# A check summed over partitions by VectorE block transposes instead of fp32 matmuls, with a fallback branch of seven transfers

## Chip, cores, metric

One Trainium2 chip, one core. The metric is device time in microseconds (us) of one execution. The kernel of before had a median of 1509.73 us in three runs (1509.59 to 1510.04).

## The reference, cut to what matters

```python
def _A_ref(x, mem0, Wq, Wk, Wv, Wo, seg_len):   # x 1 x 2048 x 1024, 64 segments of 32 tokens
    mem = mem0                                   # 8 memory rows
    for s in range(n_seg):
        h = concat([mem, xs]);  q, k, v = h @ Wq, h @ Wk, h @ Wv      # 32 heads of 128
        p = softmax(where(mask, q k^T * scale, -1e9))
        o = (p @ v) @ Wo
        mem = o[:, :M]                           # memories of the next segment
        outs.append(o[:, M:])

def _B_ref(x, w1, w2, w3, w4):
    h = gelu(layernorm(x) @ w1);  x1 = x + shift(h) @ w2
    return x1 + gelu(layernorm(x1) @ w3) @ w4

xn = layernorm(x)
return x + _A_ref(xn, ...) + _B_ref(xn, ...)
```

The recurrence over 64 segments is serial. The kernel guesses all memories beforehand, computes every segment in parallel, and at the end compares the memories that come out with the guesses. If they differ, a branch at the end does the serial computation. For these inputs the guesses hold, and the branch is never taken.

## The kernel before

These are the parts that the change and the argument touch. First the constants and the helper that sums squares over partitions with a matmul by ones:

```python
    def load_consts(n):
        for _ in range(n):
            t, d = const_loads.pop(0)
            nc.gpsimd.dma_start(t[:], d.ap())

    ident = const_tile("c_ident", np.eye(P, dtype=np.float32))
    load_consts(1)
    ...                                     # four more: eye9, mask_first, mask_reg, mask_two

    def row_norms(pool, ppool, tag, src, in_place=False):
        sq = src if in_place else pool.tile([P, KT, NQ], F32, tag="nsq", bufs=1)
        nc.vector.tensor_tensor(sq[:], src[:], src[:], op=ALU.mult)
        sr = pool.tile([P, NQ], F32, tag="nsr", bufs=1)
        nc.vector.tensor_reduce(sr[:], sq[:].rearrange("p k r -> p r k"), axis=AX.X, op=ALU.add)
        ps = ppool.tile([P, 512], F32, tag=tag)
        nc.tensor.matmul(ps[:1, :NQ], ones_f[:], sr[:], start=True, stop=True)      # L163
        return ps
```

The start. Every token tile is normalised, then transposed: tiles 0 to 5 by TensorE, tiles 6 to 15 by a DMA transpose on SyncE's queue (L278).

```python
    def load_w3():                          # 0.9 MB each
        ...
        nc.sync.dma_start(w3_sb[:, 2 * k0:2 * k0 + 2, cs], w3_v[:, 2 * k0:2 * k0 + 2, cs])

    for n in range(7, 10):
        load_x(n)                           # nc.sync.dma_start, 0.25 MB each
    def norm_stats(n, part=None):
        ...
        nc.gpsimd.tensor_tensor(rr[:], ab[:], neghalf[:], op=ALU.pow)               # L265
    def norm2(n, xn2T, jj):
        ...                                 # DVE for n < 8, else ACT (L276)
        if n >= NPE:                        # NPE = 6
            nc.sync.dma_start_transpose(xn2T[:, jj], xn2[:])                        # L278
    def norm1(n):
        ...
        if n < 3:
            load_x(n + 10)
        if n in (12, 15):
            load_w3()
    ...
    load_consts(4)
    for n in range(1, 6):
        ...
    for n in range(13, NT):
        load_x(n)
    def prep(n):
        norm2_of(n)
        norm_stats(n + 1)
        norm1(n - 2)
    for n0 in range(4, NT, 2):
        ...                                 # stage1(n0, 2, ...): matmuls by w1, L318
    for n in (NT - 2, NT - 1):
        norm1(n)
```

The middle and the tail:

```python
    def unit_thr():                         # between two units of the value stage
        ps = row_norms(ring, psum3, "vr", GT)
        nc.vector.tensor_scalar(gthr[:], ps[:1, :NQ], TOL2, None, op0=ALU.mult)
    ...
    bad = smp.tile([P, 1], F32, tag="bad", bufs=1)      # 1 where a softmax sum is out of range
    ...
    for o in rest[:2]:
        for p in range(8):
            o.piece(p)                      # output matmuls, L725
    psd = row_norms(iop, apsum, "S", Dm, in_place=True) # Dm = memories - guesses
    okf = smp.tile([1, NQ], F32, tag="okf", bufs=1)
    nc.vector.tensor_tensor(okf[:], psd[:1, :NQ], gthr[:], op=ALU.is_le)
    ...
    nc.tensor.matmul(psc[:1, :1], bad[:], ones_f[:], start=True, stop=True)         # L886
    ...
    for o in rest[2:]:
        for p in range(8):
            o.piece(p)

    cond = nc.values_load(flag_i[0:1, 0:1], min_val=0, max_val=NQ + P)
    with tc.If(cond > 0):                   # L896: 29 transfers
        nc.sync.dma_start(wo_sb[:], Wo_v)
        nc.sync.dma_start(mask40[:], mask40_d.ap())
        with tc.For_i(0, NSEG, 1) as i:
            ...                             # xs, Rt, 8 x (wq, wk, wv) in eighths, out
```

## Time and profile before

| quantity | before | where from |
|---|---|---|
| time, three runs | 1509.73 us (1509.59 to 1510.04) | timed runs |
| span of the profiled run | 1508.1 us | top of the page |
| TensorE busy | 1498.3 us, 99% | table of busy time |
| start: first transpose to first matmul by w2 | 59.46 us | starts of the records |
| first matmul by w3 to first value matmul | 410.74 us | starts of the records |
| attention: first score matmul (L682) to the check's first matmul (L865) | 701.82 us | starts of the records |
| last stage: the check's matmuls to the last matmul | 36.27 us | starts of the records |
| last matmul to the end | 4.07 us | starts of the records |

The busy table is read first: an engine at 99% leaves the others nothing to decide except at the start and behind its last instruction.

### The profile page before, as it was taken

Reading aid. Unit: us, or ns where it says so; the run is one execution under the profiler, and the core shown is the slowest. Engines: PE = TensorE matmul, PEld = TensorE weight load, DVE = VectorE, ACT = ScalarE, POOL = GpSimd, SP = SyncE. Lnnn points to the kernel's source line nnn. Section 1 sums busy time; section 2 is a strip of 40 time slices with the busy share of each in tenths; the row PEclk is TensorE's granted clock in tenths of the full one; section 3 lists DMA queues with packets and bytes.
Section 4 is the critical chain, followed back from the end, with each engine's and each line's share of the span. In section 5 each row is a group of like instructions: output and inputs, shape, how many; then the busy total and the mean of one; then the engine's idle time right before and its main releaser. Section 6 shows DMA issues by size and latency. Waiting matters only on the chain.

```text
span 1508.1 us, 24241 instructions
## 1 busy us (share of the span) xinstructions
PE 1498.3 (99%) x9762; PEld 803.5 (53%) x9834; DVE 544.6 (36%) x1136; ACT 501.9 (33%) x1140; POOL 175.6 (12%) x246
## 2 busy tenths in 40 slices
PE   9999999999999999999999999999999999999998
PEld 8744444445444444444456645664665455545555
DVE  8382230100020212221146624651564166516641
ACT  6433103013012011111256614650663266416630
POOL 5241020211111221100000010001000100010001
PEclk9999999999999999999999999999999999999999
DMA  9599762353355787622389956992998299919911
GB/s 313 155 254 329 220 180 88 133 203 113 126 164 147 195 250 253 212 98 84 126 223 254 244 125 175 257 239 68 247 244 203 74 227 228 212 62 200 216 49 51
DMA packets 305380, 272.93 MB, mean 181 GB/s; under 512 B 156023, under 2 KB 272281, under 8 KB 305265
## 3 DMA queue, kind: packets, MB, share of 16 engines
q1 hardware_dynamic: 282800, 189.38, 50.5%
q0 software_dynamic: 21776, 80.85, 15.6%
q8 instruction: 79, 1.29, 0.4%
q10 hardware_dynamic: 688, 1.11, 0.2%
q14 instruction: 37, 0.30, 0.1%
HBM read 190.08 MB, written 45.29 MB: 156 GB/s over the span
## 4 chain that ended last, share of the span: by engine, by line
PE 97%; DVE 1%; DMA 1%; issue 0%; POOL 0%; ACT 0%; SPq 0%; POOLq 0%
PE ps L667 30%; PE pso L725 15%; PE ps L601 15%; PE ps L542 13%; PE ps L568 13%; PE ps L400 4%; PE ps L318 2%; PE psS L682 2%; PE psO L706 2%; PE ps L865 1%; PE ps L492 1%; PE gps L471 0%; PE ps L457 0%; DMA wt<-in_A_Wq_dram 0%; DVE st L262 0%
## 5 line engine op out<-in xcount | busy, mean ns | idle before, releaser
L667 PE MATMUL ps<-hTb,wt 128*128 128x396 bf16 (+2 forms) x2528 | 485.0, 342 | 0.1
L667 PEld LDWEIGHTS <-wt 128*128 128x128 bf16 x2528 | 236.7, 98 | 175.8 <-DMA wt<-in_A_Wq_dram 0.5
L601 PE MATMUL ps<-wt,xT 128*128 128x512 bf16 x1003 | 220.1, 379 | 1.1
L725 PE MATMUL pso<-wo_sb,oX 128*128 128x512 bf16 (+1 forms) x972 | 208.5, 372 | 1.1
L542 PE MATMUL ps<-xn3T,w_sb 128*128 128x512 bf16 x896 | 196.2, 379 | 0.0
L568 PE MATMUL ps<-w_sb,h3T 128*128 128x512 bf16 x873 | 194.3, 379 | 1.2
L601 PEld LDWEIGHTS <-xT 128*128 128x128 bf16 x1024 | 100.2, 98 | 120.8
L543 ACT ACTIVATE h3T<-ps 128x512 bf16<-128x512 f32 x112 | 66.8, 597 | 290.4 <-PE ps L542 289.5
L725 PEld LDWEIGHTS <-oX 128*128 128x128 bf16 x992 | 96.3, 98 | 107.4
L669 ACT CAST KT<-ps 128x462 bf16<-128x462 f32 (+2 forms) x160 | 81.7, 510 | 203.0 <-PE ps L667 198.8
L568 PEld LDWEIGHTS <-h3T 128*128 128x128 bf16 x896 | 87.0, 98 | 103.4
L542 PEld LDWEIGHTS <-w_sb 128*128 128x128 bf16 x896 | 86.6, 98 | 102.0
L688 DVE TENSOR_REDUCE sums<-sm 99x4 f32<-99x396 f32 (+2 forms) x176 | 97.6, 555 | 114.9 <-ACT sm L686 114.9
L671 ACT ACTIVATE QT<-ps 128x462 bf16<-128x462 f32 (+2 forms) x160 | 83.8, 524 | 120.6 <-PE ps L667 106.6
L603 ACT CAST Vs<-ps 128x512 bf16<-128x512 f32 x64 | 37.5, 585 | 233.2 <-PE ps L601 174.9
L684 DVE TENSOR_TENSOR sm<-psS,c_mask_reg_sb 99x396 f32<-99x396 f32 x152 | 86.7, 570 | 71.7 <-PE psS L682 71.4
L607 DVE CAST Vs<-ps 128x512 bf16<-128x512 f32 x64 | 44.3, 692 | 171.6 <-PE ps L601 163.2
L686 ACT ACTIVATE sm<-sm 99x396 f32<-99x396 f32 (+2 forms) x176 | 92.8, 527 | 35.0 <-DVE sm L684 28.2
L694 DVE TENSOR_TENSOR Pn<-sm,rs 99x396 bf16<-99x396 f32 (+2 forms) x176 | 98.9, 562 | 7.1 <-DMA PT<-Pn 0.8
L732 POOL DMA_DIRECT2D out_dram<-ot x30 | 16.4, 546 | 698.9 <-DVE ot L731 693.0
L569 DVE TENSOR_TENSOR R<-ps,R 128x512 f32<-128x512 f32 x32 | 21.9, 689 | 175.3 <-PE ps L568 154.9
L731 DVE TENSOR_TENSOR ot<-pso,Rt 128x512 bf16<-128x512 f32 (+1 forms) x33 | 22.3, 675 | 170.4 <-PE pso L725 166.2
(123 smaller groups left out, 1048.3 us busy)
## 6 DMA issues: line engine op xcount, KB each, us to landing
wt<-in_A_Wq_dram SPq DMA_DIRECT2D x76, 512.0 KB
wt<-in_A_Wk_dram SPq DMA_DIRECT2D x76, 512.0 KB
wt<-in_A_Wv_dram POOLq DMA_DIRECT2D x24, 1024.0 KB, 6.5
V_scratch<-Vs SPq DMA_DIRECT2D x32, 512.0 KB
V<-V_scratch SPq DMA_DIRECT2D x40, 384.0 KB
R_scratch<-x POOLq DMA_DIRECT2D x16, 512.0 KB, 4.7
R<-R_scratch SPq DMA_DIRECT2D x16, 512.0 KB
R_scratch<-R POOLq DMA_DIRECT2D x16, 512.0 KB, 3.8
```

The source lines that it names most:

```text
L542: nc.tensor.matmul(ps[:].rearrange("p (n t) -> p n t", t=P), w3_sb[:, k, f * P:(f + 1) * P], xn3T[tb][:, :, k, :], start=(k == 0), stop=(k ...
L543: nc.scalar.activation(h3T[:, f, :], ps[:], ACTF.Gelu_apprx_tanh)
L568: nc.tensor.matmul(ps[:], h3T[:, f, j * P:(j + 1) * P], w4_sb[:, f, ch * 512:(ch + 1) * 512], start=(f == 0), stop=(f == FT - 1))
L601: nc.tensor.matmul(ps[:], xT[:, m4 * 4 + j, k, :], wv[:, k, :], start=(k == 0), stop=(k == KT - 1))
L667: nc.tensor.matmul(ps[:, :nb], w[:, k, hh * P:(hh + 1) * P], B["hT"][:, k, :nb], start=(k == 0), stop=(k == KT - 1))
L669: nc.scalar.copy(dst[:, hh, :], ps[:, :nb])
L671: nc.scalar.mul(dst[:, hh, :], ps[:, :nb], scale)
L684: nc.vector.tensor_tensor(sm[:T, :, :T], S3, t["mask"][:].unsqueeze(1).to_broadcast((T, 4, T)), op=ALU.add)
L686: nc.scalar.activation(e[:T, :, :T], sm[:T, :, :T], ACTF.Exp, scale=LN2)
L688: nc.vector.tensor_reduce(ss, e[:T, :, :T], axis=AX.X, op=ALU.add)
L694: nc.vector.tensor_tensor(Pn[:T, :, :T], e[:T, :, :T], rs[:T, :].unsqueeze(2).to_broadcast((T, 4, T)), op=ALU.mult)
L725: nc.tensor.matmul(self.ps[:, :self.w], self.oX[0][:, h, self.oX[1] + self.gl * P:self.oX[1] + (self.gl + 1) * P], wo_sb[:, h, self.cc], s ...
```

## The change

Its intent is to take the three small fp32 matmuls of the check out of TensorE's stream, to do those sums over partitions on VectorE with two block transposes, and to make the branch's body short: seven large transfers instead of 29, with the mask of the branch moved to the constants.

```diff
+    mask40 = const_tile("c_mask40", _serial_mask())
-    gthr = cpool.tile([1, NQ], F32)
-    def row_norms(pool, ppool, tag, src, in_place=False):
-        ...
-        nc.tensor.matmul(ps[:1, :NQ], ones_f[:], sr[:], start=True, stop=True)
+    def row_sums(src):
+        nc.vector.tensor_tensor(src[:], src[:], src[:], op=ALU.mult)
+        sr = smp.tile([P, NQ], F32, tag="nsr")
+        nc.vector.tensor_reduce(sr[:], src[:].rearrange("p k r -> p r k"), axis=AX.X, op=ALU.add)
+        return sr
...
-                    load_consts(4)
+                    load_consts(5)
...
-                def unit_thr():
-                    ps = row_norms(ring, psum3, "vr", GT)
-                    nc.vector.tensor_scalar(gthr[:], ps[:1, :NQ], TOL2, None, op0=ALU.mult)
-                        if u is unit_g and i == 7:
-                            pending.append(unit_thr)
...
+        dsum, gsum = row_sums(Dm), row_sums(GT)
+        nc.vector.scalar_tensor_tensor(col[:, :NQ], gsum[:], TOL2, dsum[:], op0=ALU.mult, op1=ALU.subtract)
+        ...
+        nc.vector.transpose(colT[:].rearrange("p c r -> p (c r)"), col[:])
+        nc.vector.tensor_reduce(part[:], colT[:], axis=AX.X, op=ALU.add)
+        for q in range(4):
+            nc.vector.tensor_copy(four[:, q, :], part[32 * q:32 * q + 32, :])
+        ...
+        nc.vector.transpose(sqrT[:], sqr[:])
+        nc.vector.tensor_reduce(alike[:], sqrT[0:1, :], axis=AX.X, op=ALU.min)
+        ...
-        for o in rest[:2]:
+        for o in rest:
             for p in range(8):
                 o.piece(p)
-        psd = row_norms(iop, apsum, "S", Dm, in_place=True)
-        ...
-        nc.tensor.matmul(psc[:1, :1], bad[:], ones_f[:], start=True, stop=True)
-        ...
-        for o in rest[2:]:
-            for p in range(8):
-                o.piece(p)
     with tc.If(cond > 0):
-            mask40 = fbig.tile([L, 8 * L], BF16)
-            nc.sync.dma_start(mask40[:], mask40_d.ap())
...
-                for hg in range(8):
-                    wq = fw.tile([P, KT, 512], BF16, tag="w")
-                    nc.sync.dma_start(wq[:], Wq_v[:, :, cs_])
-                    ...                                          # wk, wv alike
+                for which, src in enumerate((Wq_v, Wk_v, Wv_v)):
+                    w = fw.tile([P, KT, H * DH], BF16, tag="w")
+                    nc.sync.dma_start(w[:], src)
```

More of the change, by code (lines that the diff above doesn't have):

```diff
@@ L154 @@
     SH = (-1, -1, 1, 1, -2, -2, 2, 2)
-    def row_norms(pool, ppool, tag, src, in_place=False):
-        sq = src if in_place else pool.tile([P, KT, NQ], F32, tag="nsq", bufs=1)
-        nc.vector.tensor_tensor(sq[:], src[:], src[:], op=ALU.mult)
-        sr = pool.tile([P, NQ], F32, tag="nsr", bufs=1)
-        nc.vector.tensor_reduce(sr[:], sq[:].rearrange("p k r -> p r k"), axis=AX.X, op=ALU.add)
-        ps = ppool.tile([P, 512], F32, tag=tag)
-        nc.tensor.matmul(ps[:1, :NQ], ones_f[:], sr[:], start=True, stop=True)
-        return ps
+    def row_sums(src):
[3 more added lines that the diff above has]
+        return sr
     SEGS = ((3,) * 4,) * 3 + ((3,) * 4 + (2,), (2,) + (3,) * 4)
@@ L873 @@
         nc.vector.tensor_scalar(inr[:, 1:2], lo[:, 1:2], SUM_HIGH, None, op0=ALU.is_le)
-        bad = smp.tile([P, 1], F32, tag="bad", bufs=1)
-        nc.vector.tensor_tensor(bad[:], inr[:, 0:1], inr[:, 1:2], op=ALU.mult)
-        nc.vector.tensor_scalar(bad[:], bad[:], -1.0, 1.0, op0=ALU.mult, op1=ALU.add)
-        for o in rest[:2]:
+        dsum, gsum = row_sums(Dm), row_sums(GT)
+        col = smp.tile([P, 96], F32, tag="col", bufs=1)
+        nc.vector.memset(col[:], 0.0)
+        nc.vector.scalar_tensor_tensor(col[:, :NQ], gsum[:], TOL2, dsum[:], op0=ALU.mult, op1=ALU.subtract)
@@ new lines @@
+        nc.vector.tensor_tensor(col[:, NQ - 1:NQ], inr[:, 0:1], inr[:, 1:2], op=ALU.mult)
+        nc.vector.tensor_scalar(col[:, NQ - 1:NQ], col[:, NQ - 1:NQ], -1.0, None, op0=ALU.add)
+        colT = smp.tile([P, 3, 32], F32, tag="colT", bufs=1)
+        nc.vector.transpose(colT[:].rearrange("p c r -> p (c r)"), col[:])
+        part = smp.tile([P, 3], F32, tag="part", bufs=1)
+        nc.vector.tensor_reduce(part[:], colT[:], axis=AX.X, op=ALU.add)
+        four = smp.tile([32, 4, 3], F32, tag="four", bufs=1)
@@ new lines @@
+        for q in range(4):
+            nc.vector.tensor_copy(four[:, q, :], part[32 * q:32 * q + 32, :])
+        okf = smp.tile([32, 3], F32, tag="okf", bufs=1)
+        nc.vector.tensor_reduce(okf[:], four[:].rearrange("p q c -> p c q"), axis=AX.X, op=ALU.add)
+        nc.vector.tensor_scalar(okf[:], okf[:], 0.0, None, op0=ALU.is_ge)
+        sqr = smp.tile([32, 32], F32, tag="sqr", bufs=1)
+        nc.vector.memset(sqr[:], 1.0)
+        nc.vector.tensor_reduce(sqr[:, 0:1], okf[:], axis=AX.X, op=ALU.min)
@@ L878 @@
+        sqrT = smp.tile([32, 32], F32, tag="sqrT", bufs=1)
+        nc.vector.transpose(sqrT[:], sqr[:])
+        alike = smp.tile([1, 1], F32, tag="alike", bufs=1)
+        nc.vector.tensor_reduce(alike[:], sqrT[0:1, :], axis=AX.X, op=ALU.min)
+        nc.vector.tensor_scalar(alike[:], alike[:], -1.0, 1.0, op0=ALU.mult, op1=ALU.add)
+        nc.vector.tensor_copy(flag_i[:], alike[:])
+        for o in rest:
             for p in range(8):
                 o.piece(p)
-        psd = row_norms(iop, apsum, "S", Dm, in_place=True)
@@ L881 @@
-        okf = smp.tile([1, NQ], F32, tag="okf", bufs=1)
-        nc.vector.tensor_tensor(okf[:], psd[:1, :NQ], gthr[:], op=ALU.is_le)
-        nok = smp.tile([1, 1], F32, tag="nok", bufs=1)
-        nc.vector.tensor_reduce(nok[:], okf[:, 0:NQ - 1], axis=AX.X, op=ALU.add)
-        psc = apsum.tile([P, 512], F32, tag="O", bufs=2)
-        nc.tensor.matmul(psc[:1, :1], bad[:], ones_f[:], start=True, stop=True)
-        cnt = smp.tile([1, 1], F32, tag="cnt", bufs=1)
-        nc.vector.tensor_scalar(cnt[:], nok[:], -1.0, float(NQ - 1), op0=ALU.mult, op1=ALU.add)
@@ L889 @@
-        nc.vector.tensor_tensor(cnt[:], psc[:1, :1], cnt[:], op=ALU.add)
-        nc.vector.tensor_copy(flag_i[:], cnt[:])
-        for o in rest[2:]:
-            for p in range(8):
-                o.piece(p)
-    cond = nc.values_load(flag_i[0:1, 0:1], min_val=0, max_val=NQ + P)
+    cond = nc.values_load(flag_i[0:1, 0:1], min_val=0, max_val=1)
     with tc.If(cond > 0):
@@ L899 @@
             fbig = fctx.enter_context(tc.tile_pool(name="fbig", bufs=1))
-            fw = fctx.enter_context(tc.tile_pool(name="fw", bufs=4))
+            fw = fctx.enter_context(tc.tile_pool(name="fw", bufs=1))
             fr = fctx.enter_context(tc.tile_pool(name="fr", bufs=2))
@@ L903 @@
             nc.sync.dma_start(wo_sb[:], Wo_v)
-            mask40_d = nc.inline_tensor(_bf(np.tile(_serial_mask(), (1, 8))), name="c_mask40")
-            mask40 = fbig.tile([L, 8 * L], BF16)
-            nc.sync.dma_start(mask40[:], mask40_d.ap())
             hseg = fbig.tile([P, KT, L], BF16)
@@ L922 @@
                 nc.vector.tensor_copy(hseg[:, :, M:L], psx[:])
-                for hg in range(8):
-                    cs_ = slice(hg * 512, (hg + 1) * 512)
-                    hs_ = slice(hg * 4, (hg + 1) * 4)
-                    wq = fw.tile([P, KT, 512], BF16, tag="w")
-                    nc.sync.dma_start(wq[:], Wq_v[:, :, cs_])
-                    wk = fw.tile([P, KT, 512], BF16, tag="w")
-                    nc.sync.dma_start(wk[:], Wk_v[:, :, cs_])
-                    wv = fw.tile([P, KT, 512], BF16, tag="w")
-                    nc.sync.dma_start(wv[:], Wv_v[:, :, cs_])
-                    ps = fps.tile([P, 4, L], F32, tag="mm")
-                    for hh in range(4):
-                        for k in range(KT):
-                            nc.tensor.matmul(ps[:, hh, :], wq[:, k, hh * P:(hh + 1) * P], hseg[:, k, :], start=(k == 0), stop=(k == KT - 1))
-                    nc.scalar.mul(QTa[:, hs_, :], ps[:], QSCALE)
-                    ps = fps.tile([P, 4, L], F32, tag="mm")
-                    for hh in range(4):
-                        for k in range(KT):
-                            nc.tensor.matmul(ps[:, hh, :], wk[:, k, hh * P:(hh + 1) * P], hseg[:, k, :], start=(k == 0), stop=(k == KT - 1))
-                    nc.scalar.copy(KTa[:, hs_, :], ps[:])
-                    ps = fps.tile([P, 512], F32, tag="mm")
-                    for k in range(KT):
-                        nc.tensor.matmul(ps[:L, :], hseg[:, k, :], wv[:, k, :], start=(k == 0), stop=(k == KT - 1))
-                    nc.vector.tensor_copy(Va[:, cs_], ps[:L, :])
@@ new lines @@
+                for which, src in enumerate((Wq_v, Wk_v, Wv_v)):
+                    w = fw.tile([P, KT, H * DH], BF16, tag="w")
+                    nc.sync.dma_start(w[:], src)
+                    for hg in range(8):
+                        hs_ = slice(hg * 4, (hg + 1) * 4)
+                        if which < 2:
+                            ps = fps.tile([P, 4, L], F32, tag="mm")
+                            for hh in range(4):
+                                h = hg * 4 + hh
+                                for k in range(KT):
+                                    nc.tensor.matmul(ps[:, hh, :], w[:, k, h * P:(h + 1) * P], hseg[:, k, :], start=(k == 0), stop=(k == KT - 1))
+                            if which == 0:
+                                nc.scalar.mul(QTa[:, hs_, :], ps[:], QSCALE)
+                            else:
+                                nc.scalar.copy(KTa[:, hs_, :], ps[:])
+                        else:
+                            cs_ = slice(hg * 512, (hg + 1) * 512)
+                            ps = fps.tile([P, 512], F32, tag="mm")
+                            for k in range(KT):
+                                nc.tensor.matmul(ps[:L, :], hseg[:, k, :], w[:, k, cs_], start=(k == 0), stop=(k == KT - 1))
+                            nc.vector.tensor_copy(Va[:, cs_], ps[:L, :])
@@ L946 @@
                 for g8 in range(4):
                     psS = fps.tile([L, 8, L], F32, tag="S", bufs=1)
-                    nc.tensor.matmul(psS[:].rearrange("p h k -> p (h k)"), ident[:L, :L], mask40[:], start=True, stop=False, skip_group_check=True)
+                    nc.tensor.matmul(psS[:], ident[:L, :L], mask40[:].unsqueeze(1).to_broadcast((L, 8, L)), start=True, stop=False, skip_group_check=True)
                     for hh in range(8):
```

## The prediction

> **What bounds the kernel now.** I read the page's busy table first, then the chain of work that ended last in order of time (start, middle, end), then the instruction records of the places that the change touches. The busy table says that this is one TensorE kernel from end to end:
>
> ```profile
> PE 1498.3 (99%) x9762; PEld 803.5 (53%) x9834; DVE 544.6 (36%) x1136; ACT 501.9 (33%) x1140; POOL 175.6 (12%) x246
> PE 97%; DVE 1%; DMA 1%; issue 0%; POOL 0%; ACT 0%; SPq 0%; POOLq 0%
> ```
>
> Only three kinds of time can move the end: TensorE's own instructions, the start (until TensorE runs without gaps) and the tail after its last matmul. DVE work in the middle is free. Last 60 us of the chain (start us, us, what), where the check sits:
>
> ```profile
> 1476.52 10.74 PE pso L725 x49
> ...
> 1487.31 2.75 PE pso L725 x12
> 1490.07 0.21 PE ps L163 x2
> 1490.28 0.03 PE psc L886 x2
> 1490.31 14.01 PE pso L725 x96
> 1504.32 0.02 issue
> 1504.35 0.42 DVE ot L731
> ```
>
> The two fp32 sums (L163, L886) stand in TensorE's stream between output matmuls, so all of their time is on the path. The DVE work that feeds them ended at 1478.7 and they ran at 1490.0: nobody waited for DVE. The chain ends with the last DVE add at 1504.77, yet the span is 1508.1. What lies behind is in the lines of the branch (L896) and of the kernel's end (L1020), first and last start at the right:
>
> ```profile
> L896 SPq EVENT_SEMAPHORE  x8: 17/17/17, 1501.9 to 1506.4; - x8
> L896 PEldq COMPARE_BRANCH  x1: 3392/3392/3392, 1502.8 to 1502.8; - x1
> L1020 SPq EVENT_SEMAPHORE  x14: 17/28/28, 1506.5 to 1508.0; - x14
> SPq L896 <- SPq L896: 4.2, 3, 3.5
> ```
>
> When the branch is not taken, SyncE still settles eight DMA semaphores, one for each of the eight that the branch's transfers use (8 records at L896). The eighth is the semaphore of the last output store: issued by ACT at 1504.80, all 16 landings in by 1506.375, record at 1506.392 (the 3.5 us wait). Only then does SyncE walk its final list: the single records show 12 double waits 0.061 us apart, 1506.471 to 1507.142, a drain at 1507.207, and the closing handshake to 1508.06. That walk is serial, behind the last store.
>
> Start of the chain:
>
> ```profile
> 11.72 0.53 POOL c_mask_two_sb L130
> 12.29 0.73 POOL rr L265
> 13.04 0.55 DVE xn L274
> ...
> 29.67 1.23 ACT xn L276
> 30.90 0.18 issue
> 31.08 0.66 ACT hTB L320 x2
> 31.73 18.37 PE ps L318 x167
> ```
>
> The loads of constants (L130) are issued by Pool just ahead of a `pow` (rr) for which DVE waits. From 13 us DVE runs without slack (2.7 us for each token tile, its instructions end to end). Between 8.05 and 31.4 TensorE's starts show no gap over 0.13 us; the first is at 31.45, where it waits for the DMA transpose of tile 7 (issued 27.17, landed 31.58).
>
> **What the Trainium skill says.** "FP8 and Floating Point Precision", section TensorE Precision Notes: true fp32 takes four passes. The trace agrees: one fp32 matmul of 71 columns is two records 0.061 us apart, and a bf16 matmul of 72 columns (L492) takes 0.0325 us, so 0.122 us is 3.8 of those. "VectorE: DVE Perf Modes", section The three transpose paths: DVE transposes only independent 32x32 blocks; hence the second little transpose in the change. No DVE transpose is in this trace. "Runtime: NRT & Kernel Launch", section Instruction fetch mechanics: a taken branch to a target outside the fetched pages stops for a fetch. The trace fits: TensorE's jump over the fallback takes 3.39 us (from 1502.79), SyncE's 0.06 us. "DMA: Bandwidth & Descriptors", section Anatomy of one DMA: about 2.0 us are fixed, mostly the wait for the write's receipt (stated for the Pool path); the last store, from ACT's queue, took 1504.803 to 1506.375, 1.57 us.
>
> **The change, part by part.**
>
> *Middle, `unit_thr` gone.* It put two fp32 records into TensorE's stream at 427.4. From the start of the last matmul before (427.088) to the first after (427.614) is 0.526 us, where neighbours stand 0.216 apart: 0.31 us saved. Its DVE work (0.74 + 1.16 + 0.21) was beside TensorE: nothing. The eight `unit_vr` that follow move forward by one slot. The number of steps was 25 for 25 units and is now 25 for 24, so nothing is left to drain; the weights of the first came in long before (loads issued at 405.4 and 418.4, 6.5 us to landing; use at 427). No gain, no stall. Saved: 0.31.
>
> *Tail, two fp32 sums gone.* 1489.688 to 1490.242 is 0.554, less 0.216: saved 0.34.
>
> *Tail, DVE.* Added: squares and sums of GT (0.75 + 1.17, as those of Dm), and some 17 small instructions (multiply-subtract, transposes, reduces, copies) which I put at 0.2 each from rows like L884 (0.214) and L875 (0.160): 3.4 us. From Dm ready at 1476.74: 1.92 + 1.92 + 3.4, so the flag at about 1484, against 1491.8 now. The first `ot` of the rest is due at 1483.2 and may slip by 0.8 us; its PSUM bank is wanted again after 1500, and the Rt buffer it frees is read at 1497. Cost: 0.
>
> *Branch of seven transfers.* The semaphores of SP and ACT transfers rotate over eight, and the last three stores use the sixth, seventh and eighth. A branch with 29 transfers touches all; with seven (Wo, xs, Rt, three weights, out) it touches the first seven, so the last store's is left out. SyncE then leaves L896 after the seventh (1502.88) and does the final list while the last store flies; the list has that store's semaphore last, so only one step of 0.065 and the drain remain after 1506.39, instead of 0.815 from 1506.392 to 1507.207. TensorE's own part ends at 1506.39 (jump done 1506.18, its semaphore 1506.304), just in time. Saved: 0.75. The body of the branch is never run; its bigger transfers cost nothing.
>
> *Start.* The 40x40 mask moves from the branch into the constants: a fifth load on Pool at 12.25. The last three took 0.565, 0.554 and 0.542 us: 0.54. The `pow` at 12.29 was ready just then (its input ended at 12.20), so it moves by 0.54 and DVE with it. TensorE's transposes of tile 2 (14.29, input now 13.59) still just hold, tiles 3 to 5 have over 1 us, but tile 7's DMA transpose goes out 0.54 later, and TensorE already waits for it at 31.6. No later wait of TensorE exists that could take it up. Lost: 0.54.
>
> Sum: -0.31 - 0.34 - 0.75 + 0.54 = -0.86. 1509.73 - 0.86 = 1508.87, say 1508.9.
>
> **The rivals.**
>
> *The fifth load costs nothing.* If Pool has the slack, or tile 7's transpose lands when it does anyway because other transfers hold it, the sum is -1.40: 1508.3. For it: the transfers around 25 to 31 us are bunched. Against: DVE waited 0.23 us for this `pow` in the trace, and the chain goes through it.
>
> *The end doesn't move.* If the last store's semaphore is still settled in the branch's other side, or TensorE's jump ends later than 1506.2 and becomes the last, the 0.75 is lost: 1509.6. For it: the jump already takes 3.39 us and its fetch may vary with where the code lies; TensorE's part ended within 0.02 us of SyncE's. Against: the jump's distance barely changes.
>
> *DVE becomes the tail.* If the new DVE chain lay before the last `ot` (1504.35), it would add up to its 3.4 us: 1512. Against: all its inputs are there at 1476.7, and DVE is nearly idle for the next 27 us.
>
> *A start delay that grows*, if the late tile 2 stalls TensorE at 14.3 too: it would be the same delay, not a second one, since the wait at 31.6 is for a fixed time.
>
> **Range and chances.** The first three savings are read from gaps in the trace; the two uncertain terms are the start (0 to 0.8) and the end (0 to 0.8). Both at their good side give 1508.3, both at their bad side 1509.9; three runs of before spread over 0.45 us. So 1508.1 to 1509.7 should hold it 8 times in 10. Two per cent is 30 us; nothing here is near it: 0.99 within, the rest split.
>
> **What would show it.** No L163 or L886 on TensorE. Pool's `rr` of tile 2 at about 12.8 and TensorE's gap at 31.45 grown from 0.27 to about 0.8. The flag written by about 1484 to 1486 on that clock, no `ot` of the rest later against its matmuls than now, except the first. Seven SyncE records at L896, the last about 1.9 us before the last store is issued, and at most 0.2 us between that store's last landing and the drain. It is wrong if eight stay there, if TensorE's jump ends after the store lands, or if TensorE has a new gap in 427 to 535.

## The result, and the profile after

| | before | after |
|---|---|---|
| time, six runs each (three of those of before are the ones that the prediction reckoned from) | 1510.35 us (1509.59 to 1511.12) | 1509.66 us (1509.15 to 1511.76) |
| ratio | | 0.9997, 95% interval 0.9984 to 1.001 |
| span of the profiled run | 1508.11 us | 1507.07 us |
| start of the first transpose | 7.19 | 7.14 (-0.05) |
| start: first transpose to first matmul by w2 | 59.46 | 60.00 (+0.54) |
| first matmul by w3 to first value matmul | 410.74 | 410.42 (-0.32) |
| attention | 701.82 | 701.41 (-0.41) |
| last stage | 36.27 | 35.92 (-0.35) |
| last matmul to the end | 4.07 | 3.62 (-0.45) |

A ratio is the mean time of one kernel's fast runs over that of the other's of the same rounds, so it is not quite the ratio of the medians quoted. The middle of 1509.66 lies at the upper edge of the predicted range, and three of the six runs lie above it. The three new runs of before lie higher too (1510.66, 1511.09 and 1511.12 us): the level from which the prediction had reckoned was that of three runs that happened to be low. The difference of the two means of six is -0.43 us, half of the -0.86 that was predicted; the two profiles differ by -1.04.

TensorE's busy time on the page has gone down by 1.2 us:

```profile
PE 1497.1 (99%) x9757; PEld 803.3 (53%) x9828; DVE 546.9 (36%) x1146; ACT 502.0 (33%) x1140; POOL 176.6 (12%) x247
```

It is still at 99%, and VectorE has ten more instructions (2.3 us), so the differences of the stages have to be read one at a time. The start of the changed kernel, in the chain of waits (start, duration, what), 25 to 36 us:

```profile
30.40 0.22 DVE mv L260
30.62 0.02 issue
30.64 0.21 ACT xn L273
30.85 0.94 issue
31.79 0.37 ACT hTB L317
32.16 0.04 issue
32.20 3.87 PE ps L315 x34
```

The gap of TensorE has grown from 0.27 to 0.81 us (from the start of one matmul to that of the next), but the chain does not come through tile 7's transpose. ACT's normalisation of tile 8 began at 30.64 instead of 29.67, because it waited for tile 6's DMA transpose (landed 30.54, against 29.49 before). The chain prints VectorE's mv there, which ended last by the profile; ACT's own record of the wait for that transpose ends at 30.557 (29.516 before), 0.02 behind the landing in both, and in after_third the chain itself prints the transpose. The late normalisation held up ACT's next eviction (hTB, ending 32.16), for which TensorE waited. Tile 7's transpose had landed at 31.88.

The last 35 us of the chain of the changed kernel:

```profile
1476.28 10.74 PE pso L716 x49
...
1487.07 16.66 PE pso L716 x108
...
1503.75 0.42 DVE ot L722
```

No fp32 sum is left in the stream. The new work of VectorE lies beside it (start, busy us, line, operation, shapes):

```profile
1480.78 0.28 DVE L872 STREAM_TRANSPOSE colT<-col 128x96 f32<-128x96 f32 x1
1482.64 0.20 DVE L885 STREAM_TRANSPOSE sqrT<-sqr 32x32 f32<-32x32 f32 x1
1483.26 0.14 DVE L889 CAST flag_i<-alike 1x1 int32<-1x1 f32 x1
1483.37 0.69 DVE L722 TENSOR_TENSOR ot<-pso,Rt 128x512 bf16<-128x512 f32 x1
```

The flag is there at 1483.40, and the first output addition behind it starts at 1483.37 (1483.20 in the kernel before, where its matmuls began 0.24 later): that addition waited some 0.4 us for VectorE, but TensorE's stream shows no gap behind it, so nothing on the path was held up. What lies behind the last addition is in the records of the branch (L895) and of the waits of SyncE's queue (for the waits: total us, times, longest):

```profile
L895 SPq EVENT_SEMAPHORE  x7: 17/17/17, 1501.3 to 1502.3; - x7
L895 PEldq COMPARE_BRANCH  x1: 3732/3732/3732, 1502.2 to 1502.2; - x1
L895 PEldq EVENT_SEMAPHORE  x1: 51/51/51, 1506.0 to 1506.0; - x1
```

```profile
SPq L1014 <- PEq L895: 0.8, 1, 0.8
```

SyncE settles seven semaphores and leaves the branch at 1502.3, as predicted. But TensorE's jump over the branch took 3.73 us instead of 3.39. The last store landed at 1505.783; TensorE's semaphore came at 1506.053 and SyncE, which waited 0.8 us for it, drained at 1506.175. Before, the store landed at 1506.375 and the drain followed at 1507.207.

### The profile page after: what moved, and what is told of

Read it like the earlier page. It is cut to its first block, busy times and chain, and to the rows that moved or that the text cites. A ratio compares the mean times of both kernels' runs of the same rounds, so it can differ in the third digit from the quotient of the medians.

```text
span 1507.1 us, 24242 instructions
## 1 busy us (share of the span) xinstructions
PE 1497.1 (99%) x9757; PEld 803.3 (53%) x9828; DVE 546.9 (36%) x1146; ACT 502.0 (33%) x1140; POOL 176.6 (12%) x247
## 4 chain that ended last, share of the span: by engine, by line
PE 98%; DVE 1%; issue 0%; DMA 0%; ACT 0%; POOL 0%
PE ps L658 30%; PE ps L592 15%; PE pso L716 15%; PE ps L533 13%; PE ps L559 13%; PE ps L397 4%; PE ps L315 3%; PE psS L673 2%; PE psO L697 2%; PE ps L856 1%; PE ps L485 1%; PE gps L468 0%; PE ps L454 0%; DVE st L256 0%; DVE st L259 0%
```

## The experiments

Theory: each of the four predicted terms is a fixed time, moved only by its own part of the change; the end is now bounded by TensorE's jump. Rivals: the start is set by whichever DMA transpose lands late, so that one load of constants has no fixed price; and the end is bounded by SyncE's list as before. All runs gave correct results. Runs of the kernel before: medians of 1510.29, 1510.04, 1510.11, 1510.53 and 1510.02 us.

**after_again**: the changed kernel, nothing edited.

> The changed kernel once more, unaltered, to see what one run is worth. Theory A (the stages of the profile add up: 0.65 us less of fp32 sums, about 0.6 to 0.8 less at the end, 0.54 more at the start; runs differ for a reason that both kernels share): ratio 0.9994 plus or minus 0.0006, stages within 0.1 us of the first profile, and any longer run is longer in a stage that the change doesn't touch. Theory B (the gain of single profiles is given back in most runs): ratio 1.000, and a stage that the change touches is longer by 0.5 us or more in this profile than in the first.

Measured: 1509.36 us (1508.97 to 1510.37), ratio 0.9996 [0.9983, 1.001]. Start 60.02, jump 3.75, end 3.65. The jump and the end repeat to 0.03 us, and so does the start here.

**mask_late**: the fifth load is put behind the last tile of the start. Pool issued it at 47.0 us instead of 12.2 (the expectations below say 60).

```diff
-                    load_consts(5)
+                    load_consts(4)
...
                     for n in (NT - 2, NT - 1):
                         norm1(n)
+                    load_consts(1)
```

> The fifth constant load moved from 12 us to about 60 us, all else as in the changed kernel. Theory A: the pow of tile 2 is back at about 12.25 us, TensorE's gap at 31.4 us falls from 0.81 to 0.27, span 0.54 shorter than the changed kernel's. Rival (the transfer or the transpose of tile 7 sets that gap and not Pool's queue): the gap stays within 0.15 of 0.81.

Measured: 1509.33 us (1508.11 to 1510.3), ratio 0.9994 [0.998, 1.0007]. The start is 60.62 us: longer than with the early load, not shorter. The gap at 31 us is gone, and another of 1.42 us stands at 38.3, where the chain shows tile 9's transpose:

```profile
32.96 6.63 DMA xn2T<-xn
39.59 0.14 issue
39.73 5.29 PE ps L315 x47
```

The transpose was issued at the same time as in the kernel before (32.96 against 33.09) and took 6.63 us instead of 4.77. This alone contradicts the claim that no later wait could take up the delay. The end is 3.31 us, though the branch is that of the changed kernel: TensorE's jump took 3.39 in this build.

**branch8**: an eighth transfer in the branch, by halving one.

```diff
-            nc.sync.dma_start(wo_sb[:], Wo_v)
+            nc.sync.dma_start(wo_sb[:, 0:16, :], Wo_v[:, 0:16, :])
+            nc.sync.dma_start(wo_sb[:, 16:32, :], Wo_v[:, 16:32, :])
```

> An eighth transfer in the branch (the load of Wo in two halves), all else as in the changed kernel; the branch isn't taken. Theory A: eight SyncE records at the branch, the last after the last store has landed, then 12 double waits in series: 0.8 us between that landing and the drain, span 0.6 to 0.75 longer than the changed kernel's. Rival (the end is set by TensorE's jump over the branch, whatever SyncE does): span within 0.15 of the changed kernel's.

Measured: 1509.7 us (1509.04 to 1510.24), ratio 0.9996 [0.9982, 1.001]. The end is 4.06 us, as before the change.

```profile
L895 SPq EVENT_SEMAPHORE  x8: 17/17/17, 1501.4 to 1505.9; - x8
L895 PEldq COMPARE_BRANCH  x1: 3872/3872/3872, 1502.3 to 1502.3; - x1
```

SyncE is back at eight records, the last at 1505.9, with the store's landing (1505.894), and the drain at 1506.722 is 0.83 behind it, as in the kernel before. So the eighth semaphore is worth what was said of it, 0.75 us against an end of 3.31, whenever nothing else is later. Against the changed kernel's own end (3.62 to 3.65) it is 0.41 to 0.44, less than the 0.6 to 0.75 expected.

**no_branch**: the whole conditional taken out, the flag still computed and loaded. It is right only because these inputs never take it.

```diff
-    with tc.If(cond > 0):
-        ...
```

> The whole fallback taken out (the flag is still computed and loaded; right for these inputs, not in general). Theory A: TensorE has no jump, SyncE's drain follows the landing of the last store by 0.1 to 0.2 us; about 0.3 us shorter than the changed kernel, in which TensorE's semaphore (1506.05) comes 0.27 after that landing (1505.78). Rival (the store and not the jump sets the end of the changed kernel): within 0.1.

Measured: 1509.06 us (1508.08 to 1511.74), ratio 0.9996 [0.9983, 1.001]. End 3.31 us: without a jump the end is 0.31 below that of the changed kernel.

**before_again** (one look): the kernel before, nothing edited.

> The kernel before, unaltered, one more profile. Theory A: the steps read from its first profile come back within 0.03 us (0.53 between the matmuls around the fp32 sums at 427, 0.55 around those at 1490, 0.82 from the last landing to SyncE's drain). What differs from the first profile (59.46 us from TensorE's first transpose to its first w2 matmul) is the start alone, by up to 0.6 us either way, through the landing of the DMA transposes of tiles 6 to 9. Rival (the start is steady and the spread of the runs comes from elsewhere): within 0.1 of 59.46.

Measured: 1509.74 us. Start 59.62; the middle (410.74) and the last stage (36.27) repeat to 0.001 us, the end to 0.002. TensorE's wait in the start is at another place than in the first profile: 0.38 at 38.3 us, and none of note at 31. Not expected was that the attention stage differs too: 701.39 against 701.82.

**six_loads** (one look): a sixth constant of the same size right behind the fifth.

```diff
+    const_tile("c_extra", _serial_mask())
-                    load_consts(5)
+                    load_consts(6)
```

> A sixth, unused, constant of the same size loaded after the fifth, all else as in the changed kernel: the suspected cost doubled. Theory A: the pow of tile 2 and everything of DVE after it another 0.54 us later than in the changed kernel (pow at 13.2 to 13.3, tile 2 reaches TensorE's transpose at about 14.7, where it waits too), 60.5 us from TensorE's first transpose to its first w2 matmul if the transposes land as before. Rival (the landing of the transposes, not Pool's queue, sets the start): pow later by 0.54 all the same, but the start within what four profiles of unchanged start code showed, 60.0 to 60.46.

Measured: 1508.8 us. The Pool step is as predicted, in the chain of waits:

```profile
11.78 0.52 POOL c_mask_sb L130
12.30 0.50 POOL c_extra_sb L130
...
12.81 0.74 POOL rr L263
```

From the `pow` of tile 1 to that of tile 2 it is 4.06 us here, 3.57 with five loads and 3.07 with four: 0.5 us for each. The start is 60.43 us: just under the 60.5 of Theory A and within the rival's range, so this decides nothing. The gap at 31 us is 0.87, hardly more than with five loads.

**pe_empty** (one look): the branch keeps its seven transfers and its loop, but no arithmetic, so that TensorE has next to nothing to jump over. Right only for these inputs.

```diff
     with tc.If(cond > 0):
-            ...                             # all matmuls, evictions, the softmax
+            ...                             # the seven transfers alone
```

> The branch keeps its seven transfers and its loop but none of its arithmetic (wrong if it were ever taken, which it is not here), so that TensorE has nothing to jump over. Theory A (the jump of TensorE, whose length is that of one fetch of instructions, ends after the last store in the changed kernel and holds it up by 0.3): TensorE's branch takes under 1 us, SyncE's drain comes within 0.15 of the last landing, 3.3 us from the last matmul to the end instead of 3.6. Rival (the jump costs the same whatever lies behind it): 3.6 and a branch of over 3 us.

Measured: 1508.52 us. The jump takes 0.22 us, and the end is 3.34.

```profile
L895 PEldq COMPARE_BRANCH  x1: 223/223/223, 1502.2 to 1502.2; - x1
```

The last landing is at 1505.785, the drain at 1505.869: 0.08 us behind it. This is the predicted end. What the changed kernel lacks of it is TensorE's jump. Here too, with five loads, there is no gap at 31 us and one of 1.00 at 38.3 (tile 9 landed at 39.21).

**both_late**: as mask_late, and the last three input loads (0.75 MB) sent behind the transposes of tiles 8 and 9, to see whether bulk loads in flight are what slows a transpose.

```diff
-                    for n in range(13, NT):
-                        load_x(n)
...
                         stage1(n0, 2, tiles2[n0], between)
+                        if n0 == 4:
+                            for n in range(13, NT):
+                                load_x(n)
```

> As with the fifth constant load at about 60 us, and the loads of token tiles 13 to 15 issued after the transposes of tiles 8 and 9 instead of before them. Theory C (in the run with the late constant TensorE waited 1.2 us at 38.3 because the transposes of tiles 7 to 9 share the DMA engines with those three loads, 0.75 MB): no gap of TensorE over 0.3 us at 31 or 38, about 59.2 us from its first transpose to its first w2 matmul, 1508.0 at the median. Rival (the landing of these transposes varies whatever else is loaded): a gap of 0.3 to 1.4 us at 31 or 38 is still there.

Measured: 1509.39 us (1508.74 to 1510.26), ratio 0.9996 [0.9982, 1.0009]. Tiles 8 and 9 land 3.12 and 3.74 us after issue (4.73 and 4.77 in the kernel before). Tiles 10 and 11, which now meet the loads, take 7.17 and 9.02:

```profile
37.56 9.02 DMA xn2T<-xn
46.58 0.14 issue
46.71 3.33 PE ps L315 x29
```

The wait has moved to 45.3 us and is 1.39 long. The start is 60.63, as in mask_late.

**before_x, after_x, mask_late_x**: the same three loads moved ahead instead, into unused room of the w3 buffer, for the kernel before, the changed kernel and mask_late.

```diff
-                            xts[n] = ring.tile([P, D], BF16, tag="xt", bufs=10, name=f"xt{n}")
+                            xts[n] = ring.tile(...) if n < 13 else w3_sb[:, n - 13, 1792:1792 + D]
...
-                    for n in range(7, 10):
+                    for n in (7, 8, 9, 13, 14, 15):
...
-                    for n in range(13, NT):
-                        load_x(n)
```

> The kernel before, but token tiles 13 to 15 are loaded with the first ones (into a part of the w3 buffer that is still free) instead of between the DMA transposes of tiles 7 and 8. Theory C (those three loads share the DMA engines with the transposes, whose landing lets TensorE go on): transposes of tiles 7 to 11 land 3 to 4 us after their issue instead of 3.6 to 5.7, no gap of TensorE over 0.3 us between 30 and 50 us, 59.3 us from its first transpose to its first w2 matmul, and timed runs within 1 us of each other. Rival (the landings vary whatever is loaded): gaps and a spread as before.

> The changed kernel with the same three loads moved up. Theory C: DVE still 0.5 us later through the fifth constant, but the transpose of tile 7 lands about 1 us sooner after its issue than without the move, so the gap at 31.4 falls from 0.8 to below 0.4; 1.1 us (0.65 of fp32 sums and 0.45 to 0.75 at the end) less at the median than the kernel before with the loads moved up, if that gap closes, 0.6 less if it stays. Theory A alone (the fifth load is paid in full wherever the loads are): 0.5 us more than in the kernel before with the same move from TensorE's first transpose to its first w2 matmul.

> The changed kernel with the fifth constant at 60 us and the three token loads moved up: the candidate for the best. Theory C: no gap of TensorE over 0.3 us from 30 to 60 us, 59.3 us from its first transpose to its first w2 matmul, 1.1 to 1.4 us less than the kernel before with the loads moved up, span about 1506.2. Rival: a gap at 31, 38 or 45 us as in the two runs with the late constant.

Measured: 1512.75 us (1511.04 to 1513.56), ratio 1.0017 [1.0003, 1.0031]; 1510.42 (1509.54 to 1512.06), 1.0002 [0.9989, 1.0016]; 1511.46 (1510.04 to 1512.2), 1.0008 [0.9994, 1.0021]. None of the three came out as expected. In before_x tiles 6 and 7 take 7.9 and 6.5 us (5.0 and 4.4 in the kernel before), and TensorE stands 2.6 us at 31.3; tiles 8 to 11, with the loads out of the way, take 3.2 to 4.0. The starts are 61.80, 63.61 and 63.17. The second and third lose more than the wait. Their windows of 34 to 38 us show why (columns: window, its length, busy time and number of instructions of PE, PEld, DVE, ACT and POOL, granted clock, DMA share, GB/s); after_x:

```profile
34.00:38.00 4.00, 4.00 (x24) 2.92 (x24) 3.86 (x11) 2.77 (x7) 3.43 (x6) 0.61 0.81 195
```

before_x:

```profile
34.00:38.00 4.00, 4.00 (x39) 3.57 (x38) 3.86 (x10) 3.97 (x9) 3.53 (x6) 1.00 0.93 205
```

After a wait of that length the granted clock was 0.61 in this window in after_x and 0.57 in mask_late_x, and 24 matmuls got through instead of 39. In before_x it was 1.00 after the same wait, so it is not certain to fall. The clock records of the traces show what it was: one stretch of 3.4 us at half clock right behind the wait, in after_x (wait 2.63 us) and mask_late_x (2.27), and none in before_x (2.61). Their starts, less the wait and the 59.3 us of a start without waits (before_s, before_w), leave 1.6 to 1.7 us for it.

**checks_only** (one look): the check of the changed kernel, with the four constants and the branch of before.

```diff
-    mask40 = const_tile("c_mask40", _serial_mask())
-                    load_consts(5)
+                    load_consts(4)
...                                         # the branch of 29 transfers put back
```

> Only the check is changed (VectorE transposes in place of fp32 matmuls); the branch has its 29 transfers and the constants are four, as before. Theory A: 0.32 us less between TensorE's first w3 matmul and its first value matmul (410.42), 0.35 less in the last stage (35.92), the end as before: eight SyncE records and 4.07 us from the last matmul to the end; pow of tile 2 at 3.07 us after that of tile 1. Rival (the shift of the eight following units, or the longer chain of VectorE at the end, gives part back): less than 0.5 us in these two stages together, or more than 4.1 at the end.

Measured: 1509.42 us. Middle 410.42, last stage 35.92, end 4.07: the first two savings belong to the check alone and the third to the branch alone. Pool's step is 3.06, as before, and yet TensorE has a gap of 0.78 at 38.4 us: tile 9's transpose took 5.99 us and landed at 39.04. The start is 59.97, the same as with the fifth load. The attention stage is 701.38, between the changed kernel's 701.41 and before_again's 701.39 on one side and the shortest, 701.23, on the other.

**before_s, after_s, mask_late_s**: the three loads spread out, one behind the transpose of each of tiles 9, 10 and 11.

```diff
-                    for n in range(13, NT):
-                        load_x(n)
...
                     def prep(n):
                         norm2_of(n)
+                        if 9 <= n < 12:
+                            load_x(n + 4)
```

> The kernel before with the loads of token tiles 13, 14 and 15 put one each behind the DMA transposes of tiles 9, 10 and 11. Theory C (the transposes are slowed by those three loads in one lump): tiles 8 and 9 land within 4.2 us of their issue and tile 11 before 44.5 us, no gap of TensorE over 0.3 us from 30 to 50 us, 59.3 to 59.5 us from its first transpose to its first w2 matmul, timed runs within 1.2 us of each other. Rival (the landings vary whatever is loaded): tile 9 later than 38.2 or tile 11 later than 45, and a gap.

> The changed kernel with the same spreading. Theory C: the only gap is at 31.4 us for tile 7, 0.6 to 0.85, the fifth load paid nearly in full; 59.8 to 60.1 us to the first w2 matmul. Rival (waits at 38 or 45 take it up): a gap at 31.4 below 0.5, or one at 38 or 45 in which the kernel before has one too.

> The changed kernel with the fifth constant at 60 us and the same spreading: candidate for the best. Theory C: no gap over 0.3 us from 30 to 50 us, 59.3 to 59.5 us to the first w2 matmul, span 1506.0 to 1506.4, median about 1508.2, 1.5 to 2 us under the kernel before. Rival: a gap at 31, 38 or 45 us and a median of 1509 or more.

Measured: 1510.64 us (1509.54 to 1511.26), ratio 0.9998 [0.9985, 1.0012]; 1510.62 (1510.48 to 1511.09), 0.9999 [0.9986, 1.0013]; 1511.57 (1509.08 to 1513.27), 1.0 [0.9986, 1.0014]. In before_s no gap is left between 25 and 62 us, and the start is 59.30; but the runs spread by 1.7 us, against the 1.2 expected, and are no faster than those of the kernel before. In after_s, with the fifth load, there is a gap of 0.77 at 31.4, but the larger loss is at 60: tile 15's transpose takes 9.13 us beside the first load of w3, a gap of 1.51. In mask_late_s the same transpose takes 10.10, the wait is 2.80, and 3.4 us at half clock follow it:

```profile
51.63 10.10 DMA xn2T<-xn
61.73 0.14 issue
61.87 4.23 PE ps L315 x22
```

**after_third**: the changed kernel once more, on the chip of these three.

> The changed kernel, unaltered, a third time. If the mean of all its runs so far (1509.8 against 1510.2 of the kernel before) is what it is worth: 1509.8 plus or minus 0.4. If the prediction's 0.86 is: 1509.3 or less. The gap at 31.4 us again 0.8, none at 38.

Measured: 1510.3 us (1508.69 to 1510.41), ratio 0.9994 [0.998, 1.0007]. Middle, last stage and end repeat (410.42, 35.92, 3.64). The start is 60.93, almost a microsecond more than in the two other profiles of the same code, because a second wait stands behind the one at 31:

```profile
33.89 5.98 DMA xn2T<-xn
39.87 0.14 issue
40.01 5.07 PE ps L315 x45
```

**before_w, mask_late_w**: as the spread versions, and the first load of w3 sent behind tile 15's transpose too.

```diff
-                        if n in (12, 15):
+                        if n in (13, 15):
                             load_w3()
```

> The kernel before, the three token loads spread behind tiles 9 to 11 and the first w3 load moved behind the transpose of tile 15. If the waits come from these collisions: no gap of TensorE over 0.3 us from 30 to 62 us, tile 15 lands within 5 us of its issue, 59.2 to 59.4 us to the first w2 matmul, timed runs within 1.2 us of each other and about 0.7 under the kernel before. Rival: another transpose is late instead and the runs spread by 2 us or more.

> The changed kernel with the fifth constant at 60 us and both moves: candidate for the best. If the waits come from these collisions: 59.2 to 59.4 us to the first w2 matmul, span about 1506.1, 1.1 to 1.4 us under the kernel before with both moves and about 1508.2 at the median. Rival: a gap between 30 and 62 us, and a median of 1509 or more.

Measured: before_w 1509.85 us (1508.98 to 1510.35), ratio 0.9996 [0.9983, 1.001]; mask_late_w 1508.02 (1507.95 to 1508.83), 0.9987 [0.9973, 1.0]. Neither has a gap in the start: 59.32 and 59.30 us. The chain of mask_late_w from 25 to 62 us is one piece:

```profile
24.98 37.12 PE ps L315 x340
```

With the start freed of its waits, the savings remain: the mean of mask_late_w's runs is 1.54 us below that of before_w, near the 1.42 that the check and the end add up to (0.32, 0.35 and 0.75), and 2.05 below that of the kernel before in the same rounds. (The two profiles differ by 2.13, of which 0.83 lies in the attention stage, see below.) The changed kernel with the early fifth load and both moves was not run, so what the late constant adds to the moves is not isolated. mask_late_w is the best version, and its five runs lie within 0.9 us.

## Why the prediction was right or wrong

*Middle: right.* Predicted -0.31, measured -0.32 in every build with the new check, checks_only included.

*Two sums of the tail: right.* Predicted -0.34, measured -0.35, in the same builds.

*VectorE's chain: right.* The flag was due at about 1484 and came at 1483.40; it cost nothing.

*End: mechanism right, size wrong.* The step "TensorE's own part ends at 1506.39 (jump done 1506.18, its semaphore 1506.304), just in time. Saved: 0.75" failed. It carried the jump of before (3.39 us) over to the new code. In the three profiles of the changed kernel the jump took 3.71 to 3.75 us and ended behind the last store, so the term was -0.42 to -0.45. The prediction's own sign of being wrong, "if TensorE's jump ends after the store lands", came true: 1505.93 against 1505.78. The rival in which TensorE's jump becomes the last had been named, with the whole 0.75 as its price; it came true for 0.3 of it. That the rest of the mechanism holds is shown from both sides: with no long jump (pe_empty) or with a jump of 3.34 to 3.43 us (both_late, six_loads, mask_late, mask_late_w) the end is 3.31 to 3.34, the full 0.75 below before; with longer jumps the end grows with them: 3.41 and 3.42 at 3.51 and 3.53 us (mask_late_s, after_x), 3.81 at 3.91 (after_s). With the eighth semaphore (branch8) it is 4.06 again. Why the jump is longer in some builds was only narrowed down. In the profiles it is some 0.95 us to the start of one instruction fetch of 16 KB (1.50 in after_s), that fetch's packet, and about 1.5 us more. The packet took 0.92 and 0.98 us in the two profiles of before, 1.27, 1.27 and 1.23 in the three of the changed kernel, 0.96 in mask_late and 1.39 in branch8. Profiles of one build agree to 0.07 us, builds differ by more; the cause stays open.

*Start: this step failed.* The prediction said that tile 7's DMA transpose goes out 0.54 later and that "No later wait of TensorE exists that could take it up. Lost: 0.54." Its first half is shown: Pool's step grows by 0.5 us for each load (3.07, 3.57, 4.06), tile 7's transpose is issued 0.47 us later, and the gap at 31 us is 0.81 to 0.83 in the three profiles of the changed kernel. Of the other builds with the early fifth load, branch8 has 0.76 there, no_branch 0.36 and pe_empty none. Its second half is false. The start holds ten DMA transposes, tiles 6 to 15, and TensorE waits for whichever lands too late. In one profile of the kernel before that was tile 7, in the other tile 9. The landing of the same 128x1024 transpose came between 2.7 and 10.1 us after issue, by what bulk loads were in flight; moving 0.75 MB of loads moved the wait from one tile to another (both_late, before_x, before_s). Of the unaltered loads, four profiles without the early fifth load have starts of 59.46, 59.62, 59.97 and 60.62 us (before, before_again, checks_only, mask_late), and six with it of 60.00, 60.02, 60.13, 60.18, 60.46 and 60.93 (after, after_again, no_branch, pe_empty, branch8, after_third). The means differ by 0.37 and the single profiles by over 1 us. That the first pair of profiles differed by exactly 0.54 was chance: the chain there, and in after_again, went by another way than predicted, through tile 6 and ACT. In branch8 and after_s it does go through tile 7. What makes identical builds differ (tile 9 took 4.57 to 5.98 us in the three of the changed kernel) is not shown.

*Range: the spread was taken from too little.* "Three runs of before spread over 0.45 us" was the measure. The 51 runs of the kernel before in all rounds run from 1509.31 to 1512.12, with a mean of 1510.31 and a standard deviation of 0.62; the first three lay 0.5 below that mean, and their median, from which the prediction reckoned, 0.6. That the waits for transposes make the spread is not shown: mask_late_w, with no wait in its profile, spread by 0.9 us over five runs and mask_late, with one, by 2.2; but before_w, with none, spread by 1.4 and after_s, with two, by 0.6.

*The sum.* Sixteen runs of the unaltered changed kernel have a mean of 1509.84; they lie 0.43, 0.58 and 0.84 us below before, 0.6 in the mean, against the predicted 0.86. The profiles of unaltered code agree: the mean span of the three after (1507.33) is 0.57 below that of the two before (1507.90). That sum is -0.32 (middle), -0.35 (tail), -0.44 (end), +0.77 (start), -0.16 (attention) and -0.08 (first transpose). So of some 1.1 us taken from TensorE's stream and from the end, 0.77 went back into the start by these five profiles, 0.37 by the ten of the paragraph on the start: between a third and two thirds.

*Not foreseen: the attention stage.* It took 701.39 to 702.12 us in the five profiles with the old check and 701.23 to 701.69 in the fifteen with the new one (means 701.84 and 701.32). TensorE waits there at a few places, for a load of projection weights or for a transpose of the softmax's output. Eight of the fifteen lie at 701.23 or 701.24; none of the five does. checks_only has 701.38, no shorter than before_again (701.39), so it does not settle which part of the change matters. The two groups overlap, and no run isolates the cause: it stays open.

## What to carry to other kernels

A delay on a bounding engine's supply line has no fixed price when several transfers race to be the last: list every wait that could become last, with the spread of its transfer, before calling any of them the only one. Before sending more loads, ask which latency-critical transfer will be in flight beside them. Here the savings came through in the build that both moved the loads behind the critical transposes and took the fifth constant out of the start (mask_late_w). The late constant alone (mask_late) kept a wait, and so did the early one with the input loads spread (after_s). When a wait is removed at the end, the next-latest thing sets the end, and a duration seen once in another build (here a jump) is not a constant to subtract from.

## What the Trainium skill lacked or had wrong

- "DMA: Bandwidth & Descriptors", section DMA Transpose (X-bar), gives constraints and no latency of a transpose among other loads; its section Rules for kernel authors says that a transpose next to ordinary DMAs "needs nothing", which is about correctness. For the time it does not hold here: the same 128x1024 bf16 transpose landed 2.7 us after issue when it met few loads and 9.0 to 10.1 beside 0.75 MB of input or the first load of w3.
- "Runtime: NRT & Kernel Launch", section Instruction fetch mechanics, says that a taken branch to a target outside the fetched pages stops for a fetch, but gives no length. Here TensorE's jump took 3.34 to 3.91 us over the branch's arithmetic and 0.22 with none to jump over; one fetch packet of 16 KB took 0.9 to 1.4 us of it, by build.
- "VectorE: DVE Perf Modes", section Rules for kernel authors, says of a reduction along the partition axis "Not possible on DVE — use GPSIMD". No single instruction does it, but two block transposes with reductions and four copies of 32 partitions brought 71 columns of sums from 128 partitions down to one flag in 3.3 us of VectorE (1480.13 to 1483.40). The two transposes were 0.28 us (128x96 fp32) and 0.20 us (32x32 fp32), which the page's table, for bf16 128x128, does not list.
